# Attention products on four 64x64 quarters of TensorE's array, with q loaded like k and v

## The chip, the cores and the metric

One core of one Trainium2 chip. The metric is the time of one execution on the device in microseconds (us); lower is better. Times are medians over the runs of a kernel.

## The reference, cut to what matters

```python
# q, k, v: (8 batches, 8 heads, 576 rows, 64), float32
kv  = np.einsum('bhsd,bhse->bhde', k, v)            # a 64x64 matrix per batch and head
out = np.einsum('bhsd,bhde->bhse', q, kv)
rms = np.sqrt(np.mean(out * out, axis=-1, keepdims=True) + 1e-06)
x   = out / rms * g_norm                            # then (8*576 rows, 512 columns)
# after it: logits = x @ w_gate, a balanced routing of the 4608 rows to 8 experts
# of 576 rows each, and relu(x @ w1[e]) @ w2[e] for the rows of expert e
```

The attention comes first, then a search that settles the routing, then the experts. Only the attention (until 183 of 791 us) is touched by the change, but for a permuted index of w1 among the experts.

## The kernel before: the parts that the change and the argument touch

Two batches are a "stage". A stage makes kv of its two batches, then runs nine "tokens" (each 128 rows of output, both batches side by side) in three groups of three. The "mark" of a stage is the start of the w_ps products (kv times the gate's weights) of its second batch. A "record" is one matmul in the trace; some records can be missing. In the views PE is TensorE, DVE VectorE, ACT ScalarE and POOL GpSimd.

```python
def load_q(i):                                   # two halves of 64 partitions
    t = att.tile([P, H, R, D], FT, name="q_sb", tag="q")
    for n, eng in enumerate((nc.sync, nc.gpsimd)):
        eng.dma_start(t[n * HP:(n + 1) * HP]..., q[2 * i + n]...)

def kv_product(b):                               # two quarters: l = row and column half
    for r in range(NP):
        for j in range(R):
            for l in range(2):
                ls = slice(l * D, (l + 1) * D)
                nc.tensor.matmul(kv_ps[ls, r, :], lhsT=k_sb[ls, r, j, :], rhs=v_sb[ls, r, j, :], ...)
    nc.vector.tensor_copy(bd[0:D, b, :, 0:D], kv_ps[0:D])
    nc.scalar.copy(bd[D:P, b, :, D:P], kv_ps[D:P])
    # [cut: t_ps = transpose of bd, kvt = copy of it, w_ps = kvt times the gate, copied into bd]

def token_group(i, j0):
    nc.gpsimd.tensor_copy(q_rows, q_sb[...])
    for t in range(T):
        # [cut: 4 transposes of q_rows into qt_ps]
        nc.vector.tensor_copy(qt, qt_ps)
        for r in range(NP):
            for n in range(2):
                nc.tensor.matmul(o_ps[ps_, r, 0:W], lhsT=qt[:, r, ps_], rhs=bd[:, 2 * i + n, r], ...)
        nc.scalar.activation(sq, o_ps[...], ACT.Square, ...)
        nc.scalar.copy(o_sb[:, t], o_ps[:, :, 0:W])
        nc.vector.reduce_sum(out=ms[...], in_=sq, ...)
    # [cut: inv = 1 / rms; x_sb = o_sb * inv on GpSimd; part, lg on VectorE; write of x_sb]

for i in range(B // 2):
    for b in (2 * i, 2 * i + 1):
        kv_product(b)                            # the loads of b + 2 follow
    for j0 in range(0, R, T):
        token_group(i, j0)
        # [cut: early(...): parts of the routing that can be done by now, on VectorE]
```

## Time and profile before

| | before |
|---|---|
| median, range of 4 runs beside the changed kernel | 791.94 us, 789.05 to 792.72 |
| mean granted TensorE clock of the profiled run | 0.945 |
| second w_ps of each stage begins | 44.1, 79.8, 119.9, 153.4 us |
| first comparison of the full routing search | 183.2 us |

The prediction below reads the chain, the stretches and the groups. First, TensorE's groups in one stage, 79.80 to 119.92 us (busy us and mean ns of one, then idle time before them):

```profile
L264 PE MATMUL kv_ps<-v_sb,k_sb 64*64 64x64 f32 x288 | 12.5, 258 | 0.0
...
L288 PE MATMUL qt_ps<-ident,q_rows 128*128 128x128 f32 x36 | 5.4, 282 | 0.0
```

Second, in the waits of the same stretch, the longest (total, times, longest one):

```profile
PE t_ps L270 <- ACT bd L267: 5.0, 1, 5.0
```

Third, the granted clock in the page's 40 slices of 20 us each; the first nine digits are the attention:

```profile
PEclk9998979985569999999999999999999999999998
```

### The profile page before, as it was taken

The numbers are of one execution on the slowest core, as the hardware profiler recorded it, in microseconds if no ns is written. First come the engines' busy times: TensorE is split into PE (matmuls) and PEld (weight loads), VectorE is DVE, ScalarE is ACT, GpSimd is POOL, SyncE is SP. The second block draws the span as 40 slices with busy tenths as digits, with TensorE's granted clock in tenths as the row PEclk, the third lists the DMA queues.
The fourth block names the chain that finished last, engine by engine and source line by source line (L and its number), as shares of the span: only waits on it lengthen the run. The fifth ranks groups of instructions, "written<-read, shape, count | busy, mean of one in ns | idle before, by whom it ended". The sixth has DMA issues, their size and how long they took to land.

```text
span 791.0 us, 10903 instructions
## 1 busy us (share of the span) xinstructions
PE 681.3 (86%) x4361; PEld 443.4 (56%) x4361; DVE 344.7 (44%) x1214; ACT 151.1 (19%) x310; POOL 138.3 (17%) x118
## 2 busy tenths in 40 slices
PE   0588878951069999999999999999999999999994
PEld 0578767840047546745754674476467547646741
DVE  0364746587825625562663455165445514000000
ACT  0041504340021112102110310221031122103200
POOL 3133514230020030013003001300310032010001
PEclk9998979985569999999999999999999999999998
DMA  8999784221240080045008102600710176110001
GB/s 220 288 265 306 223 261 161 81 81 41 88 184 1 14 299 21 1 139 194 1 1 298 34 1 104 222 7 1 272 60 1 62 265 230 50 40 21 1 27 33
DMA packets 36786, 90.89 MB, mean 115 GB/s; under 512 B 2944, under 2 KB 2944, under 8 KB 36736
## 3 DMA queue, kind: packets, MB, share of 16 engines
q1 hardware_dynamic: 29056, 66.59, 25.4%
q0 software_dynamic: 6976, 23.60, 9.2%
q8 instruction: 34, 0.56, 0.3%
q10 hardware_dynamic: 704, 0.02, 0.1%
q14 instruction: 16, 0.13, 0.1%
HBM read 71.32 MB, written 18.87 MB: 114 GB/s over the span
## 4 chain that ended last, share of the span: by engine, by line
PE 59%; issue 19%; DVE 11%; DMA 5%; ACT 2%; POOL 2%; POOLq 0%; ACTq 0%; DVEq 0%
PE h_ps L552 27%; PE y_ps L563 16%; PE o_ps L295 4%; DMA v_sb<-in_v_dram 4%; PE kv_ps L264 3%; PE y_ps L571 3%; DVE part L315 2%; PE n_ps L364 1%; DVE ms L300 1%; PE qt_ps L288 1%; DVE over L238 1%; PE w_ps L275 1%; POOL out_dram L535 1%; PE t_ps L530 1%; ACT xt L531 1%
## 5 line engine op out<-in xcount | busy, mean ns | idle before, releaser
L552 PE MATMUL h_ps<-xt,w_sb 128*128 128x288 f32 x1024 | 270.8, 415 | 0.0
L563 PE MATMUL y_ps<-w_sb,hid 128*128 128x512 f32 x512 | 227.2, 597 | 0.0
L552 PEld LDWEIGHTS h_ps<-xt,w_sb 128*128 128x128 f32 x1024 | 188.8, 191 | 52.0 <-issue 5.7
L563 PEld LDWEIGHTS y_ps<-w_sb,hid 128*128 128x128 f32 x512 | 94.8, 190 | 105.2 <-issue 104.3
L535 POOL DMA_INDIRECT out_dram<-y_sb,ids x40 | 39.7, 993 | 441.3 <-ACT y_sb L566 390.7
L576 DVE TENSOR_TENSOR y_sb<-y_ps,y_part 64x512 f32<-64x512 f32 x8 | 5.5, 683 | 208.2 <-ACT y_part L575 208.2
L555 ACT ACTIVATE hid<-h_ps 128x288 f32<-128x288 f32 x128 | 52.5, 410 | 220.0 <-PE h_ps L552 218.5
L238 DVE TENSOR_TENSOR over<-mx,cand 128x1152 bf16<-128x1152 f32 (+3 forms) x52 | 67.0, 1289 | 1.6
L566 ACT COPY y_sb<-y_ps 128x512 f32<-128x512 f32 x32 | 18.7, 585 | 209.2 <-PE y_ps L563 171.7
L295 PE MATMUL o_ps<-bd,qt 128*64 128x144 f32 x576 | 46.4, 304 | 10.8 <-DVE qt L290 9.9
L506 POOL DMA_INDIRECT xg<-x_dram,ids x40 | 39.4, 986 | 83.1 <-issue 43.7
L295 PEld LDWEIGHTS o_ps<-bd,qt 128*64 128x64 f32 x576 | 38.7, 144 | 14.7 <-ACT o_sb L299 7.9
L264 PE MATMUL kv_ps<-v_sb,k_sb 64*64 64x64 f32 x1152 | 45.2, 242 | 0.1
L264 PEld LDWEIGHTS kv_ps<-v_sb,k_sb 64*64 64x64 f32 x1152 | 42.4, 156 | 3.2 <-issue 2.9
L310 POOL TENSOR_TENSOR x_sb<-o_sb,inv 128x1536 f32<-128x1536 f32 x12 | 33.2, 2768 | 50.0 <-DVE inv L308 37.0
L364 PEld LDWEIGHTS <-over 128*128 128x128 bf16 x441 | 18.1, 97 | 38.4 <-DVE over L238 22.4
L370 DVE TENSOR_TENSOR need<-goal,n_ps 32x8 f32<-32x8 f32 x49 | 7.5, 154 | 69.0 <-PE n_ps L364 69.0
L364 PE MATMUL n_ps<-best,over 128*128 128x32 bf16 x441 | 19.2, 178 | 21.4 <-DVE cand L358 12.5
L530 PE MATMUL t_ps<-ident,xg 128*128 128x128 f32 (+1 forms) x160 | 24.0, 288 | 15.3 <-issue 10.5
L385 DVE SCALAR_TENSOR_TENSOR at<-row_f,k_ps,cand 128x33 f32<-128x33 f32 x98 | 21.5, 257 | 34.3 <-PE k_ps L380 34.3
L531 ACT ACTIVATE xt<-t_ps,g_col 128x512 f32<-128x512 f32 (+1 forms) x40 | 24.0, 645 | 53.0 <-PE t_ps L530 52.9
L530 PEld LDWEIGHTS t_ps<-ident,xg 128*128 128x128 f32 (+1 forms) x160 | 18.0, 149 | 24.9 <-issue 15.1
(149 smaller groups left out, 506.4 us busy)
## 6 DMA issues: line engine op xcount, KB each, us to landing
w_sb<-in_moe_w_dram SPq DMA_DIRECT2D x16, 1024.0 KB, 6.1
w_sb<-in_moe_w_dram SPq DMA_DIRECT2D x8, 2048.0 KB, 14.2
k_sb<-in_k_dram SPq DMA_DIRECT2D x8, 1152.0 KB
v_sb<-in_v_dram SPq DMA_DIRECT2D x8, 1152.0 KB
x_dram<-x_sb SPq DMA_DIRECT2D x12, 768.0 KB, 3.3
q_sb<-in_q_dram POOLq DMA_DIRECT2D x4, 1152.0 KB
q_sb<-in_q_dram SPq DMA_DIRECT2D x4, 1152.0 KB, 27.8
xg<-x_dram,ids POOLq DMA_INDIRECT x40
```

Of the source, the lines that this page charges most:

```text
L238: nc.vector.tensor_tensor(over[:, c0:c1], mx[:, c0:c1].rearrange("p (c o) -> p c o", o=1).to_broadcast([P, c1 - c0, NCAND]), cand[:, 1:NCA ...
L264: nc.tensor.matmul(kv_ps[ls, r, :], lhsT=k_sb[ls, r, j, :], rhs=v_sb[ls, r, j, :], start=(j == 0), stop=(j == R - 1))
L295: nc.tensor.matmul(o_ps[ps_, r, 0:W], lhsT=qt[:, r, ps_], rhs=bd[:, 2 * i + n, r], start=True, stop=True)
L310: nc.gpsimd.tensor_tensor(x_sb.rearrange("p (a l d) -> p a l d", l=2, d=D), o_sb.rearrange("p t r w -> p (t r) w")[:, :, 0:P].rearrange("p ...
L364: nc.tensor.matmul(n_ps, lhsT=over[:, c:c + G].rearrange("p c n -> p (c n)"), rhs=best[:, c:c + G].rearrange("p c e -> p (c e)"), start=(c ...
L506: nc.gpsimd.indirect_dma_start(out=xg[0:nr, :], out_offset=None, in_=x_dram, in_offset=bass.IndirectOffsetOnAxis(ap=ids[0:nr, n:n + 1], ax ...
L530: nc.tensor.transpose(t_ps[:, d, 0:nr], xg[0:nr, d * P:(d + 1) * P], ident[0:nr, 0:nr])
L531: nc.scalar.mul(xt[:, :, a:a + nr], t_ps[:, :, 0:nr], g_col)
L535: put = nc.gpsimd.indirect_dma_start(out=out, out_offset=bass.IndirectOffsetOnAxis(ap=ids_of[t][0:nr, n:n + 1], axis=0), in_=y_sb[0:nr, :] ...
L552: nc.tensor.matmul(h_ps, lhsT=w1[:, d, f * P:(f + 1) * P], rhs=xt[:, d, cs], start=(d == 0), stop=(d == DC - 1))
L555: nc.scalar.activation(hid[:, f, cs], h_ps, ACT.Relu)
L563: nc.tensor.matmul(y_ps, lhsT=hid[:, f, a:a + nr], rhs=w2[:, f, :], start=(f == 0), stop=(f == FC - 1))
```

## The change

The intent: use all four 64x64 quarters at once for kv and for the output products, so that they cost half; put the same kv into both partition halves so that q can be transposed as it lies after a load over all 128 partitions; drop GpSimd's rearrangement of q and some of VectorE's copies; let x_sb start behind part and lg, one token at a time, as part was slow when it started after x_sb. The transposes of q move out of the tokens into the preparation of a batch. The core of the diff (cut: names, assertions, the same copies in another shape, and a permuted index of w1 among the experts):

```diff
-    def load_q(i):                      # two halves of 64 partitions
+    def load(name, b):                  # k, v and q alike, 128 partitions, one queue
+        nc.sync.dma_start(t.rearrange("p r j d -> p r (j d)"),
+            src[b].rearrange("h s d -> (h s) d").rearrange("(r p j) d -> p r (j d)", r=NP, j=R))
 def kv_product(b):
-                    nc.tensor.matmul(kv_ps[ls, r, :], lhsT=k_sb[ls, r, j, :], rhs=v_sb[ls, r, j, :],
+                    ls, cs = slice(l * D, (l + 1) * D), slice(j % 2 * D, (j % 2 + 1) * D)
+                    nc.tensor.matmul(kv_ps[cs, l, r * D:(r + 1) * D], lhsT=k_sb[ls, r, j, :], rhs=v_sb[ls, r, j, :],
-        nc.vector.tensor_copy(bd[0:D, b, :, 0:D], kv_ps[0:D])
-        nc.scalar.copy(bd[D:P, b, :, D:P], kv_ps[D:P])
+        nc.scalar.copy(odd, kv_ps[D:P, :, 0:NP * D])
+        nc.vector.tensor_tensor(kv, kv_ps[0:D], odd, op=AL.add)       # even and odd j
+        nc.scalar.copy(kvx[0:D, :, 0:D], kv)
+        nc.gpsimd.tensor_copy(kvx[D:P, :, 0:D], kv)                   # kv in both halves
         # t_ps, kvt, w_ps as before in other shapes
+    def turn_q(b):                      # 18 transposes of 128x128, four to a bank
 def token_group(i, j0):
-        nc.gpsimd.tensor_copy(q_rows, ...); 4 transposes and a copy per token
-        nc.gpsimd.tensor_tensor(x_sb..., o_sb..., inv...)         # three tokens at once, ahead of part
+        for t in range(T):                                        # behind part and lg
+            nc.gpsimd.tensor_tensor(x_sb[:, t], o_sb[:, t, :, 0:D], inv...)
+            for r2 in range(NP // 2):   # o products: row half by block, column half by batch
+                for l in range(2):
+                    for rp in range(2):
+                        for n in range(2):
+                            nc.tensor.matmul(o_ps[n * HP:(n + 1) * HP, rp, ...], lhsT=turned_q[...][rows, ...],
+                                             rhs=kv_of[2 * i + n][rows, 2 * r + l], ...)
 for i in range(B // 2):
     for b in (2 * i, 2 * i + 1):
         kv_product(b)
+            turn_q(b)
```

## The prediction

> **What bounds the kernel now.** I read four views: the chain of waits, the table of stretches, the groups by shape for the first 180 us, and the timeline. The chain first, because it says how much of the 791 us the change can reach at all:
>
> ```profile
> 6.84 29.95 DMA v_sb<-in_v_dram
> 36.83 4.42 PE kv_ps L264 x144
> 44.07 1.00 PE w_ps L275 x8
> ...
> 79.80 1.08 PE w_ps L275 x8
> ...
> 119.92 1.08 PE w_ps L275 x8
> ...
> 153.35 1.08 PE w_ps L275 x8
> ...
> 177.72 2.09 DVE lg L225
> 183.22 1.36 DVE over L238
> ```
>
> Columns: start, length, what. These w_ps lines are the last small products before the nine tokens of each of four stages (two batches each), so they are a clock for the attention: 44.1, 79.8, 119.9, 153.4, periods of 35.7, 40.1 and 33.5 us. It ends near 183, where the routing search starts. The 608 us after that are experts, whose code the change does not touch but for a permuted index of w1. So only some 183 us can move. Its first part is a wait for loads: kv of the second batch waits for v until 36.8.
>
> Next, what the stretches say of the loads (busy PE, then the granted clock, DMA share and GB/s at the end of each line):
>
> ```profile
> 12.00:18.00 6.00, 0.00 (x0) 0.00 (x0) 0.00 (x0) 0.00 (x0) 0.00 (x0) 1.00 1.04 244
> 72.00:78.00 6.00, 6.00 (x129) 5.74 (x129) 0.64 (x2) 0.08 (x1) 0.00 (x0) 0.70 0.97 350
> 126.00:132.00 6.00, 5.69 (x83) 4.38 (x79) 5.71 (x10) 3.99 (x8) 2.59 (x1) 1.00 0.00 0
> ```
> ```profile
> 36.83:41.17 4.34, 4.34 (x144) 4.27 (x144) 1.00 1.04 400
> 45.50:47.60 2.10, 0.00 (x0) 0.00 (x0) 1.00 1.05 193
> ```
>
> The engines are full in all but one of these, yet move 400 GB/s or 193. By issue order k and v are under way in the fast stretch and a q half in the slow one. So q is the slow load. After 126 us the DMA is idle in stretches and the last stage still takes 33 us: the late stages are bound by compute. That compute is a serial prologue (kv product, its copies and transpose, w_ps) followed by tokens, where VectorE is fullest (5.7 to 6.0 us in every stretch of 6 us inside tokens).
>
> ```profile
> L264 PE MATMUL kv_ps<-v_sb,k_sb 64*64 64x64 f32 x1152 | 45.2, 242 | 0.1
> L290 DVE COPY qt<-qt_ps 128x512 f32<-128x512 f32 x36 | 24.4, 683 | 6.4 <-PE o_ps L295 5.2 <-PE qt_ps L288 1.1
> L300 DVE TENSOR_REDUCE ms<-sq 128x8 f32<-128x512 f32 x36 | 24.3, 675 | 6.1 <-ACT sq L298 6.1
> L315 DVE TENSOR_TENSOR part<-o_sb,inv 128x192 f32<-128x192 f32 x12 | 19.7, 1640 | 0.1
> ```
> ```profile
> 143.67 0.36 DVE L315 TENSOR_TENSOR part<-o_sb,inv 128x192 f32<-128x192 f32 x1
> 143.87 2.78 POOL L310 TENSOR_TENSOR x_sb<-o_sb,inv 128x1536 f32<-128x1536 f32 x1 [3.77 <-DVE inv L308]
> ...
> 163.47 2.76 POOL L310 TENSOR_TENSOR x_sb<-o_sb,inv 128x1536 f32<-128x1536 f32 x1 [9.69 <-DVE inv L308]
> ...
> 163.75 2.69 DVE L315 TENSOR_TENSOR part<-o_sb,inv 128x192 f32<-128x192 f32 x1
> ```
>
> The last pair is worth a look: the same part takes 0.36 us when it starts before GpSimd's x_sb and 2.69 us when it starts after it. Its mean of 1.64 us is mostly waiting.
>
> **What the Trainium skill says.** "SBUF — State Buffer", section "Door 1: The DMA port swizzle": partitions 0 to 63 reach 8 of the 16 ports, measured there at 196 GB/s against 328 for 128 partitions. The trace agrees: 193 against 400 as a q half of 64 partitions or k and v of 128 are under way. The same page, "Who interferes with whom": a VectorE instruction with two SBUF inputs contends with a GpSimd instruction that reads SBUF, and whoever issues first holds the pair for the whole instruction. The 0.36 and 2.69 us above agree. "TensorEngine Tiling (Array Packing)", "Tiling Modes": 64x64 gives four tiles that work independently, and a change of mode drains the array. "TensorE: Matmul & The Clock Gate", Part 3: concurrent tiles cost about one matmul plus 4 ns for each further one. Of these the trace shows two tiles only: 144 kv records in 4.42 us, 30.7 ns each, at 218 ns recorded length.
>
> **The change part by part**, for one stage (two batches, nine tokens).
>
> *Loads.* The same 7.08 MB of k, v and q and 2.36 MB of writes. The two q halves cost about 1.18 MB / 0.195 = 6 us each; q as 128 partitions at 380 GB/s costs 3. Loads and writes now: 4.72/0.38 + 12 + about 7 = 31 us a stage; afterwards 7.08/0.38 + 7 = 26 us. At the start it is on the path. VectorE and TensorE both begin with gw, which landed at 25.6 us behind k0, v0, both q halves and k1 (5.9 MB). In the built program only k0, v0, q0 and k1 (4.7 MB) are ahead of it: 2.5 + 4.72/0.37 = about 15.3 us. v1 lands at about 19 and q1 at 22, against v1 at 36.8.
>
> *kv.* 288 records at 30.7 = 8.8 us now. On four quarters a pitch near half, 16 to 20 ns with issue cost: 5.2 us, so 3.6 us less. Added behind it on the path of each batch: the copy of the odd half on ScalarE (64x512, estimated 0.6 from the similar copies) and an add on VectorE (the 64x512 add of the experts takes 0.68), in place of two bd copies of 0.41 and 0.37. That is +0.5 a batch. The 8 w_ps records become 16 of half the columns, about equal time. kvx copies lie beside them.
>
> *q.* The 36 transposes at 0.137 remain 4.9 us of TensorE, but move from between the tokens into the prologue: the built order shows all of a batch's 18 ahead of the first full token. Of the copies out of PSUM 3 of 5 go to VectorE (0.68, 0.68, about 0.42), so 3.6 us a stage against 6.1, and 2.4 us go to ScalarE. GpSimd's q_rows copies (3 x 1.5) are gone.
>
> *Tokens.* VectorE now: 9 x (0.68 + 0.68) + 3 x (1.64 + 0.49 + about 0.86 for inverse and corrections) = 21.2 us. After: 9 x 0.68 + 3 x (0.36 + 0.49 + 0.86) = 11.2 us, because inv, part and lg stand next to each other in the built order and x_sb starts behind part. ScalarE: two passes per token start 1.02 us apart in all, 9 x 1.02 + 3 x 0.32 = 10.1 us. o_ps: 32 records of half the width on four tiles, at 20 ns 0.64 us a token, under ScalarE's pace. So tokens cost about 11 us.
>
> *One stage afterwards.* TensorE's prologue: kv 5.2, t_ps and w_ps about 3.2, q 4.9 = 13.3 us. Stalls, as the built order runs batch by batch: odd copy and add after each kv (2 x 1.5), kvt before w_ps (2 x 0.5), the first add behind the last group's chain (1): 4 to 5 us. With tokens 10 to 11: 28 us, against 33 to 40 now. DMA needs 26, so it nearly keeps up and does not bind.
>
> *Sum.* kv(0) from 15.5 to 20 (cold clock; 6.3 us now), VectorE's constants done by 21. Then add, transpose and w_ps to 24, q and kv(1) to 29, its chain and w_ps start near 32 (44.1 now). Marks at 32, 60, 88, 116. After the last mark: 16 transposes 2.2, tokens 10.5, last chain 3.5, last early choose and first search step about 5, of which the 2.1 us lg line above shrinks as x_sb is now cut into pieces of about 0.95: some 22 to 23 us where it was 29.9. End near 139, against 183: **44 us less, 792.7 - 44 = 749 us**.
>
> **Rivals.**
> 1. *The four quarters give nothing* because issue or weight loads set the pitch of 30.7 ns. For it: records of weight loads are nearly as long as the stretch (4.27 of 4.34 us). Against it: two tiles of 64 columns already run at one clock per pair near what 144 columns cost per column (32 o_ps records in 2.11 us are 66 ns, 2.15 times 30.7 for 2.25 times the columns), so the pitch follows columns, not issue. It would put back 3.6 us a stage and, as o_ps would then cost 0.98 us, little on tokens: 749 + 14 = 763.
> 2. *The bound becomes the loads*, if writes and loads queue behind each other on the one queue: three writes of a stage stand ahead of the next k load in the built order, and buffers of k and v are two. Then 30 us a stage, or 757. If instead it fills well and stalls hide, a stage falls to 25.5 and the end to 739; loads of 28.3 MB plus writes cannot do much better than 735.
> 3. *The clock.* TensorE now idles more within tokens. Before, the granted clock fell to 0.5 to 0.78 after waits, and kv of 124 records took 6.1 instead of 3.8 us. Cold prologues would add some 3 us a stage: about 760.
> 4. *Nothing comes through*, the transposes in the prologue undoing all of it: a stage of 35 us. Even then the earlier start keeps 12 us: 780, within 2%.
>
> **Range and chances.** The start (12 us) is the surest; the rest is 32 us from three stages and the end, in which each rival takes 8 to 14 and two of them may meet. I take 749, range 735 to 768. Under 777 is faster by 2%: 94%. Within 2% needs rival 4 or several together: 5%. Slower: 1%.
>
> **What would show it.** Right: first kv_ps near 16 us; GB/s of 340 to 400 in all early stretches; w_ps marks 28 us apart; kv_ps dense stretches at 16 to 20 ns a record; part at 0.36 to 0.5 us mean; qt and ms together about 11 us less VectorE; the experts' part still 608 us. Wrong: kv_ps at 30 ns (rival 1), TensorE waiting on DMA at kv_ps (rival 2), a clock under 0.8 in most of the attention (rival 3), or an experts' part that changes by more than 3 us, which nothing here explains.

## The result, and the profile after

The changed kernel takes 778.71 us (777.04 to 779.12, 4 runs) against 791.94. The ratio is 0.9836, 95% interval 0.9805 to 0.9866. A ratio here is the mean time of one kernel's fast runs over that of the other's fast runs of the same rounds, so it is not quite the ratio of the medians. About 13 us are gained, not 44; the predicted range was 735 to 768.

The start came near what was predicted. Stretches of the changed kernel (busy time of the five engines, then clock, DMA share, GB/s):

```profile
12.00:18.00 6.00, 4.41 (x146) 4.39 (x146) 4.18 (x29) 0.20 (x1) 0.00 (x0) 1.00 1.05 391
```

In this stretch the loads move 391 GB/s where it was 244, and TensorE and VectorE work where they stood still. The first kv product begins at 14.1 us (27.0 before).

The stages did not. The timeline of TensorE gives the w_ps of each stage's second batch:

```profile
31.99 0.58 PE L275 MATMUL w_ps<-gw,kvt 128*64 128x16 f32 x13 [0.59 <-ACT kvt L271]
...
69.38 1.04 PE L275 MATMUL w_ps<-gw,kvt 128*64 128x16 f32 x16
...
108.00 0.65 PE L275 MATMUL w_ps<-gw,kvt 128*64 128x16 f32 x16 [0.59 <-ACT kvt L271]
...
142.62 0.65 PE L275 MATMUL w_ps<-gw,kvt 128*64 128x16 f32 x16 [0.59 <-ACT kvt L271]
```

So the marks are 32.0, 69.4, 108.0, 142.6 where 32, 60, 88, 116 were predicted: stages of 37.4, 38.6 and 34.6 us instead of 28, and hardly different from the 35.7, 40.1 and 33.4 of before. The full search begins at 170.1 us (183.2 before), so the whole gain, 13.1 us, is the 12.1 us of the earlier first mark plus 1.0. After it nothing changed.

The stretches view of the three stages gives granted clocks of 0.81, 0.74 and 0.80. TensorE is busy in them for 25.8, 25.9 and 24.8 us. The second:

```profile
69.40:108.00 38.60, 25.93 (x642) 22.10 (x640) 21.90 (x44) 15.90 (x31) 10.69 (x11) 0.74 0.72 254
```

Where that stage goes, by TensorE's groups from 69.38 to 108.00 us:

```profile
L289 PE MATMUL qt_ps<-ident,q_sb 128*128 128x128 f32 x36 | 8.7, 413 | 0.0
L255 PE MATMUL kv_ps<-v_sb,k_sb 64*64 64x64 f32 x278 | 8.7, 260 | 0.0
L311 PE MATMUL o_ps<-kvx,qt 64*64 64x72 f32 x288 | 7.8, 245 | 4.7 <-ACT o_sb L318 4.7
...
L269 PE MATMUL t_ps<-ident,kv 64*128 64x64 f32 x8 | 1.1, 280 | 7.4 <-DVE kv L260 7.4
```

kv fell from 12.5 to 8.7 us, not to 5.2. The same 36 transposes rose from 5.4 to 8.7. TensorE stands still for 4.7 us ahead of output products and 7.4 ahead of the transpose of kv. The same view of the first and the third stage has 17.0 and 16.1 us for kv and q's transposes together, 4.6 us of waits ahead of output products in each, and 3.7 and 4.6 ahead of the transpose of kv; the second stage has the longest of these. (Overlaps make the parts of this view sum to a little more than the stage.)

The timeline shows these waits one by one (start, length, what, and in brackets the wait and what ended it):

```profile
48.33 1.24 PE L311 MATMUL o_ps<-kvx,qt 64*64 64x72 f32 x32 [2.40 <-ACT o_sb L318]
...
62.50 1.90 PE L255 MATMUL kv_ps<-v_sb,k_sb 64*64 64x64 f32 x105
...
96.04 0.68 PE L269 MATMUL t_ps<-ident,kv 64*128 64x64 f32 x4 [6.11 <-DVE kv L260]
```

The middle line is a dense stretch at a full clock: 105 records in 1.90 us, 18 ns each, inside the predicted 16 to 20. The last line is the costliest wait. VectorE's own timeline shows what it did meanwhile:

```profile
93.66 1.52 DVE L225 TENSOR_TENSOR over<-mx,cand 128x512 bf16<-128x512 f32 x1
...
95.31 0.67 DVE L260 TENSOR_TENSOR kv<-kv_ps,odd 64x512 f32<-64x512 f32 x1
```

The add that TensorE waits for (L260) stands in VectorE's program behind the last group's chain and an early part of the routing (92.26 to 95.31). Its last input, the copy odd, began at 89.98 and took 0.58 us, so it was there 4.7 us before.

And the clock, in the same slices as above:

```profile
PEclk9787777855589999999999999999999999999998
```

Sevens and eights where there were nines. A "cold" stretch is one at a granted clock near half, a "warm" one at the full clock. In a cold stretch eight q transposes take 1.97 us, in a warm one 1.09.

Three explanations offer themselves, and they do not exclude each other. **Order**: kv, the transposes and w_ps of the next stage come (but for a handful of kv products) after the tokens of this one in each engine's program, so the engines wait for each other at every seam between two stages, and each microsecond saved turns into waiting. **Clock**: the sparser TensorE runs part of the time at half rate, and loses on transposes what it gained on kv. **Loads**: two buffers of k and v keep the queue idle (7 GB/s from 42 to 48 us).

### The profile page after: what moved, and what is told of

Its sections match the earlier page's. It is cut to its first block, busy times and chain, and to the rows that moved or that the text cites. A ratio compares the mean times of both kernels' runs of the same rounds, so it can differ in the third digit from the quotient of the medians.

```text
span 777.4 us, 12187 instructions
## 1 busy us (share of the span) xinstructions
PE 659.4 (85%) x5001; PEld 420.6 (54%) x5001; DVE 329.6 (42%) x1202; ACT 164.4 (21%) x334; POOL 123.2 (16%) x132
## 4 chain that ended last, share of the span: by engine, by line
PE 51%; issue 22%; POOL 2%; DMA 2%; ACT 1%; DVE 1%; POOLq 0%; ACTq 0%
PE h_ps L572 28%; PE y_ps L583 17%; PE y_ps L591 3%; DMA xg<-x_dram,ids 2%; PE t_ps L549 1%; PE n_ps L383 1%; POOL out_dram L554 1%; ACT xt L550 1%; POOL xg L525 1%; PE k_ps L399 1%; ACT y_sb L586 0%; POOL x_sb L337 0%; DVE ms L319 0%; DVE lg L212 0%; DVE pick L216 0%
## 5 line engine op out<-in xcount | busy, mean ns | idle before, releaser
L337 POOL TENSOR_TENSOR x_sb<-o_sb,inv 128x512 f32<-128x512 f32 x36 | 37.8, 1075 | 65.8 <-DVE inv L327 34.4
L311 PE MATMUL o_ps<-kvx,qt 64*64 64x72 f32 x1152 | 31.3, 245 | 18.9 <-ACT o_sb L318 18.9
L311 PEld LDWEIGHTS o_ps<-kvx,qt 64*64 64x64 f32 x1152 | 25.1, 145 | 25.2 <-ACT o_sb L318 23.0
L383 PEld LDWEIGHTS <-over 128*128 128x128 bf16 x441 | 18.2, 97 | 36.8 <-DVE over L225 24.1
L383 PE MATMUL n_ps<-best,over 128*128 128x32 bf16 x441 | 19.2, 178 | 20.8 <-DVE cand L377 12.5
L255 PE MATMUL kv_ps<-v_sb,k_sb 64*64 64x64 f32 x1152 | 33.6, 262 | 2.5 <-DMA v_sb<-in_v_dram 2.5
L255 PEld LDWEIGHTS kv_ps<-v_sb,k_sb 64*64 64x64 f32 x1152 | 29.6, 169 | 6.7 <-issue 6.4
L289 PE MATMUL qt_ps<-ident,q_sb 128*128 128x128 f32 x144 | 32.9, 394 | 0.3 <-DVE qt L293 0.3
```

What stands on the lines that cost most here:

```text
L255: nc.tensor.matmul(kv_ps[cs, l, r * D:(r + 1) * D], lhsT=k_sb[ls, r, j, :], rhs=v_sb[ls, r, j, :], start=(j < 2), stop=(j >= R - 2))
L289: nc.tensor.transpose(t_ps[:, x, :], q_sb[:, (a + x) * P:(a + x + 1) * P], ident)
L311: nc.tensor.matmul(o_ps[n * HP:(n + 1) * HP, rp, (2 * r2 + l) * W:(2 * r2 + l + 1) * W], lhsT=turned_q[2 * i + n][rows, block // 2, l * HP ...
L337: nc.gpsimd.tensor_tensor(x_sb[:, t], o_sb[:, t, :, 0:D], inv[:, t * H:(t + 1) * H].rearrange("p (a o) -> p a o", o=1).to_broadcast([P, H, ...
L383: nc.tensor.matmul(n_ps, lhsT=over[:, c:c + G].rearrange("p c n -> p (c n)"), rhs=best[:, c:c + G].rearrange("p c e -> p (c e)"), start=(c ...
```

## The experiments

Edits are shown against the changed kernel unless said otherwise. All had three rounds beside the kernel before (medians 790.5 to 791.2 us). "Gain" is 791 us times one minus the ratio; for the changed kernel it is 13.0.

### 1. A third buffer for o_sb

```diff
-        o_sb = att.tile([P, T, H, W], FT, name="o_sb", tag="o_sb")
+        o_sb = att.tile([P, T, H, W], FT, name="o_sb", tag="o_sb", bufs=3)
```

> The changed kernel with three o_sb buffers for two; TensorE's order is the same. Theory A (the stage is a serial prologue plus tokens, with waits in it): TensorE's wait of 2.4 us at the eighth token of each stage, for o_sb held by GpSimd's x_sb, goes away: 4 x 2.4 = 9 us less, about 769 to 771, and the clock after that point is higher. Rival B (the wait only moves, to VectorE's chain or to the loads): within 2 us of 778.

Measured: 775.93 us (773.25 to 776.68), ratio 0.9797 [0.9771, 0.9824], gain 16.1. TensorE's two largest waits over three stages, 32 to 142 us, in the changed kernel:

```profile
PE t_ps L269 <- DVE kv L260: 15.7, 6, 6.1
PE o_ps L311 <- ACT o_sb L318: 13.9, 21, 2.4
```

and with the third buffer:

```profile
PE t_ps L269 <- DVE kv L260: 21.0, 6, 8.0
PE o_ps L311 <- ACT o_sb L318: 9.3, 21, 0.8
```

The wait for o_sb lost 4.6 us and the next wait in the program, for VectorE's add, grew by 5.3. The tokens ended sooner, and TensorE waited longer at the seam. That speaks for order. The time met neither expectation (769 to 771, or within 2 us of 778), and its interval overlaps that of the changed kernel (0.9805 to 0.9866), so the 3 us between them are not sure.

### 2. The writes of x on another queue

```diff
-        nc.sync.dma_start(x_dram[...], x_sb...)
+        nc.gpsimd.dma_start(x_dram[...], x_sb...)
```

> The changed kernel with the x_dram writes issued from GpSimd's queue, so that no load stands behind a write that waits for x_sb. Theory A: the 2.45 us that TensorE waits for v at 66 us goes, loads in 42 to 54 us are no longer near zero, and the time falls by 2 to 5 us to 774 to 776. Rival (the loads are not on the path): within 1 us. Against both: issuing costs GpSimd about 0.8 us a write and may delay x_sb, plus 2 us.

Measured: 778.5 us (777.3 to 779.9), ratio 0.9837 [0.9813, 0.9862], gain 12.9: nothing. k of the third stage still began to load only when kv of the stage before had been read. TensorE's wait for v stayed too (2.5 us). Writes ahead of loads on one queue are not the cause.

### 3. The kernel before with only q's load widened (wrong result)

```diff
 # against the kernel before; rows land in the wrong places
-            eng.dma_start(t[n * HP:(n + 1) * HP]..., q[2 * i + n].rearrange("h (p j) d -> p h (j d)", j=R))
+            eng.dma_start(t[:, n * NP:(n + 1) * NP]..., q[2 * i + n]...rearrange("(r p j) d -> p r (j d)", r=NP, j=R))
```

> The kernel BEFORE with only q's loads changed: each half through all 128 partitions instead of 64 (wrong result on purpose, same bytes, engines and instructions). Theory A (the 13 us gained are the earlier start by wider q loads, the rest of the change is neutral): about 779 to 782, the first mark of the stages near 34 instead of 44 us. Rival C (the loads also paced the stages before): below 775. Rival D (the start is set by gw and the number of transfers, not by their width): above 787.

Measured: 781.66 us (779.77 to 783.43), ratio 0.9872 [0.9849, 0.9896], gain 10.1. Of the 13 us of the whole change, the wide q load alone gives about 10; if the parts add, the others together gave 3. The time fits the expectation, its path only in part: the first mark came at 37.7 us (34 expected, 44.1 before, 32.0 in the changed kernel), and 3.7 us of the gain came from shorter stages after it.

### 4. Only two quarters at work at once

```diff
-            for j in range(R):
+            for j in [j for c in range(2) for j in range(c, R, 2)]:      # kv: even j, then odd j
...
-            for r2 ...: for l ...: for rp ...: for n in range(2):
+            for n, r2, l, rp in [(n, r2, l, rp) for n in range(2) ...]:   # o: one batch, then the other
```

> The changed kernel with kv's and o's products in an order in which only two quarters work at a time (same instructions, right result). If the four quarters do run together: dense kv_ps goes from 18 ns a record to about 30, o_ps from 0.73 us a token to about 1.1, and the time rises by 8 to 14 us to 786 to 792. Rival (they give nothing[...]): within 3 us of 778.

Measured: 779.78 us (775.2 to 782.44), ratio 0.9846 [0.9802, 0.9891], gain 12.2. Two dense stretches of kv:

```profile
51.85 3.04 PE L255 MATMUL kv_ps<-v_sb,k_sb 64*64 64x64 f32 x90
...
66.10 2.21 PE L255 MATMUL kv_ps<-v_sb,k_sb 64*64 64x64 f32 x98
```

The first, 34 ns a record, ran at a granted clock of 0.62; in the changed kernel 104 records at 0.65 took 2.64 us, 25 ns each. The second, at the full clock, has 23 ns where the changed kernel has 18. So two quarters cost a quarter to a third more a record, not double as expected, and less than the 30.7 ns of the kernel before: most of that fall does not come from four quarters at once, and where it comes from was not tested. A token's products take 1.04 us instead of 0.73 at the full clock.

The time rose by about 1 us, within the spread. The profile shows why the slower products cost so little: the first mark is later (35.2 us, 32.0 in the changed kernel), but from there the three stages take 108.5 us with TensorE busy for 84.9 (clock 0.76, 0.90 and 0.82), where the changed kernel takes 110.6 with 76.5. The longer busy time came out of waits. So TensorE's rate alone is not what a stage waits for.

### 5. Keeping TensorE warm

```diff
+        for _ in range(16):       # before the transpose of kv
+            nc.tensor.matmul(idle, lhsT=ones_b, rhs=inner, start=True, stop=True)          # 288 columns
...
+            for _ in range(2):    # behind each token's products, into columns that nothing reads
+                nc.tensor.matmul(o_ps[:, 0, 288:512], lhsT=ones_b, rhs=inner[..., 0:224], ...)
```

> The changed kernel with TensorE kept busy: two bf16 products of 224 columns into a part of o_ps that is overwritten or never read, behind each token's products, and sixteen of 288 columns into a spare PSUM tile in each kv product before the transpose of kv. The result stays correct. Clock theory (the faster, sparser TensorE work lets the granted clock fall, and the cold transposes, kv and o products then give back what the quarters save): the granted clock of the stages rises from 0.74-0.87 to above 0.93, eight q transposes take 1.1 us instead of 2.0, and the time falls by 6 to 12 us, to 767-773. In-order theory (the end of a stage is set by waits of VectorE and TensorE for each other in program order, not by TensorE's rate): the clock rises too, but the time stays within 4 us, 775-783, since the fillers cost about as much as warmth returns.

Measured: 776.91 us (775.28 to 778.35), ratio 0.9828 [0.9804, 0.9852], gain 13.6. The clock of the three stages rose to 0.99, 0.83 and 1.00, the mean q transpose fell from 394 to about 325 ns, and the time moved by less than 2 us. But the fillers of the first two batches delayed the first mark from 32.0 to 36.1 us, so this run was not clean, and I repeated it without them:

```diff
-        for _ in range(16):
+        for _ in range(16 if b >= 2 else 0):
```

> The changed kernel with TensorE's fillers (two small bf16 products behind each token, sixteen before the transpose of kv) but none of the sixteen in the first two batches, where they stood on the path and the first mark came at 36.1 instead of 32.0. Clock theory: first mark at 32-33, later stages as in the filler run (104 us over three stages instead of 110.6), so 770-773. If the clock is worth nothing and the filler run was only noise: 776-780.

Measured: 774.17 us (773.67 to 777.42), ratio 0.9812 [0.9784, 0.984], gain 14.9. That is 1.9 us over the changed kernel by the ratios and 4.5 by the medians, from separate calls; it falls between what the two theories expected. The three stages took 104.8 us instead of 110.6, at a clock of 0.95, 0.87 and 1.00. So warmth returned a few microseconds net. That is no upper bound of what the low clock costs: the fillers took 26 us of TensorE over the attention (12.8 and 13.3 by their groups), some of them where it would have waited, some not, and no run gives warmth without them.

### 6. Preparing the next stage between this stage's tokens

```diff
+    def prepare(b):
+        kv_product(b); turn_q(b)
+        # and the loads of b + 2
+    prepare(0); prepare(1)
     for i in range(B // 2):
-        for b in (2 * i, 2 * i + 1):
-            kv_product(b); turn_q(b)
-        for j0 in range(0, R, T):
+        for g, j0 in enumerate(range(0, R, T)):
             token_group(i, j0)
+            if g < 2 and 2 * i + 2 + g < B:
+                prepare(2 * i + 2 + g)
```

(with four buffers for kvx and qt, three for o_sb, and three for x_sb instead of six, for room)

> The changed kernel with the next stage's two kv products and q transposes written between the token groups of this stage (after the first and the second group), with four buffers for kvx and qt and three for o_sb. Same work, same instructions. In-order theory: the serial prologue (20 us between the last token product of a stage and the next w_ps mark) disappears beside the tokens; the stage period falls from 35-38 us to 26-31, what VectorE, ScalarE or the loads leave, and the time is 750-764. Clock theory: the work between tokens also keeps TensorE warm, so the run alone does not part the two, but a granted clock that stays below 0.85 together with a time under 765 would show that the clock was not it. Loads theory: the stage stays at 31 us or more with TensorE or ScalarE waiting for loads, 765-775.

Measured: 764.78 us (764.11 to 765.33), ratio 0.9669 [0.9653, 0.9685], gain 26.2, correct. The same products gain 13 us more. Not all of that is order: the third o_sb buffer alone gave about 3 (experiment 1), so some 10 remain for the order with what it needs, the further buffers of kvx and qt and the earlier loads (a batch's loads follow its preparation). TensorE waited for a load for only 2.5 us in the changed kernel, so earlier loads can hardly be the 10. The marks are 31.8, 59.8, 88.9 and 126.1: two stages of 28 and 29 us, then one of 37 in which the early routing stands in front of the add once more. The two short stages in the stretches:

```profile
32.00:60.00 28.00, 21.61 (x618) 18.60 (x617) 13.38 (x29) 13.77 (x27) 7.45 (x8) 0.84 0.77 281
60.00:89.00 29.00, 23.85 (x656) 20.78 (x657) 16.67 (x37) 15.83 (x31) 9.39 (x10) 0.80 0.85 315
```

The clock in them is 0.84 and 0.80, little above that of the changed kernel (0.81 and 0.74), so a full clock is not needed for short stages.

### 7. A third buffer for k and v (and for o_sb)

```diff
-        ... tag=name, bufs=3 if name == "q" else 2)
+        ... tag=name, bufs=3)
```

(and three buffers for x_sb instead of six, for room)

> The changed kernel with three buffers for k, v and o_sb (three for x_sb instead of six, for room). Loads theory (k(4) cannot load before kv(2) is done, so the queue is nearly idle 42-54 us and TensorE waits 2.5 us for v_sb before the w_ps mark of each stage): the wait for v_sb goes, and compared with o_sb's third buffer alone (775.9) 5 to 8 us are won, 768-771. In-order theory: the wait goes but the tokens' and VectorE's order set the stage, 773-776.

Measured: 774.23 us (773.67 to 776.6), ratio 0.98 [0.9779, 0.9821], gain 15.8: no more than o_sb's buffer alone (16.1). The expected end of the wait for v did not come (2.4 us, once, as before), because the queue now waited for q's three buffers. This run does not settle how far earlier loads could go; it shows only that a third buffer for k and v, at the price of three of x_sb, brings nothing.

### 8. Do the quarters pay once the order is right?

The edit of experiment 4 on the kernel of experiment 6.

> The version with kv and q prepared ahead (764.8), but TensorE's products ordered so that only two of the four quarters work at once (as in the run with two quarters, where kv cost 34 ns a record instead of 18-25 and a token 1.04 us instead of 0.73-1.24). If the four quarters pay once TensorE no longer stands still at the stage's end: each stage needs about 288 x 12 ns + 9 x 0.3 us = 6 us more TensorE time, of a stage of 28-29 us in which it is busy 22-24: 5 to 15 us slower, 770-780. If TensorE still has slack enough: 764-768, and the quarters are worth nothing anywhere in this kernel.

Measured: 770.76 us (770.23 to 773.28), ratio 0.9756 [0.9734, 0.9778], against 0.9669 with four quarters: 7 us slower. What made no clear difference in experiment 4 is worth 7 us here.

### 9. The same order in the kernel before

The edit of experiment 6 on the kernel before (kv products and loads only; three buffers for q).

> The kernel before with the next stage's kv products and loads written between the token groups (three buffers for q), nothing else of the change. Correct result. If the serial prologue is what hid the gain, the kernel before is held by it too, but its tokens fill VectorE (21 us a stage) and its q loads stay slow: 778-786, a gain of 5 to 13. If the prologue matters as much in it as in the changed kernel: 775-779 (14 us). If the order alone explains all of the 764.8: under 770.

Measured: 792.99 us (792.66 to 794.71), ratio 1.0025 [1.0008, 1.0042], correct. My expectation (778 to 786) was wrong: no gain at all. Its stretches suggest why:

```profile
48.00:85.00 37.00, 32.04 (x511) 27.97 (x511) 16.52 (x35) 12.80 (x25) 10.24 (x6) 0.91 0.91 252
85.00:120.00 35.00, 32.14 (x555) 27.34 (x556) 21.04 (x50) 15.06 (x29) 14.51 (x7) 1.00 0.98 316
```

TensorE is busy for 32 us of 35 to 37 and the DMA engines for over 90%: the kernel before, so ordered, has little slack to give. (Which of the two binds, no run shows; this version had no third o_sb buffer.) In these runs the order pays only together with the cheaper products and loads. The wide q load pays without the order too (experiment 3).

### 10. Two details of the reordered kernel

Two fillers of 224 columns behind each token, on experiment 6:

> The version prepared ahead with two bf16 products of 224 columns behind each token's products into columns of o_ps that nothing reads, to keep TensorE's clock up (0.80-0.84 in its stages, 0.60 in the last). Clock theory: clock above 0.9, q transposes at 1.1 us per eight instead of 1.9, 758-762. No effect of the clock: 763-768.

Measured: 766.42 us (762.83 to 768.67), ratio 0.9682 [0.9646, 0.9718]: no effect, with the clock of the three stages at 0.89, 0.92 and 0.84 (0.85, 0.80 and 0.77 without the fillers).

The early routing of 24 columns in one piece after the third stage, on experiment 6:

> The version prepared ahead with the early choice of the first 24 columns in one piece after the third stage, so that VectorE's add for kv does not stand behind it (TensorE waited 4.95 us at 119.4 and 1.7 at 105.9 for that add). In-order theory: these waits fall under 1.5 us and the third stage from 37 to 31-33 us; the time falls by 3 to 6 us, 759-762, unless the piece of choice moved to the last stage costs as much there: 764-766.

Measured: 765.4 us (763.75 to 766.25), ratio 0.9676 [0.9655, 0.9697]: no effect. The one wait of 4.95 us became one of 6.53 at the same place, as the larger piece now stood in front of the last add. The piece has to go elsewhere, or the add must not be waited for.

### 11. The next stage in small pieces between the tokens

On experiment 6: the preparation is a generator that yields after each fourth of kv and each four transposes; each token takes three pieces. q's transposes now stand between a batch's kv and the transpose of kv, so that VectorE's add has time.

```diff
     def kv_product(b):
         for r in range(NP):
             ...
+            yield
         # odd, kv, kvx
+        yield from turn_q(b)              # yields after each four transposes
         t_ps = ...
 def token_group(i, j0, ahead):
     for t in range(T):
         ...
+            for _ in range(3):
+                next(ahead, None)
```

> The version prepared ahead, but with the next stage's work cut into pieces of a fourth of a kv product or four q transposes, three pieces behind each token, and with q's transposes between a batch's kv product and the transpose of kv, so that VectorE's add has time. If what is left is waits by order (t_ps for the add, 11.6 us; stops in dense kv, 8.4 us; waits for o_sb, 6 us): these fall to under half, stages of 25-27 us, limited by loads (26) or ScalarE, and 752-760. If the stage is at the limit of TensorE's own time at this clock or of the loads: 762-766.

Measured: 753.11 us (752.9 to 754.18), ratio 0.9535 [0.9517, 0.9554], gain 36.8, correct. This is the fastest version, almost 5% below the kernel before and 3% below the changed one. It lies inside the range predicted for the change, but that is no success of the prediction, which was made for another order. Its marks in TensorE's timeline, after a first one at 30.76:

```profile
61.61 0.65 PE L278 MATMUL w_ps<-gw,kvt 128*64 128x16 f32 x16
...
90.19 0.65 PE L278 MATMUL w_ps<-gw,kvt 128*64 128x16 f32 x16
...
119.50 0.65 PE L278 MATMUL w_ps<-gw,kvt 128*64 128x16 f32 x16
```

Stages of 30.9, 28.6 and 29.3 us; the search begins at 144.8. The wait for the add is gone altogether. (I did not part the two halves of this edit, small pieces and the moved transposes.) What remains is another kind of stop:

```profile
72.74 0.90 PE L315 MATMUL o_ps<-kvx,qt 64*64 64x72 f32 x28 [4.21 <-issue]
```

"issue" means that TensorE waited for nothing that the profile shows. Such stops sum to 16.1 us between 30 and 140 us. The DMA view of the 50 ns from 70.15 us on has this line (packets, MB, share):

```profile
q8 instruction: 1, 0.02, 134.9%
```

A 16 KB packet on the queue for instructions began there (its share is over 100% because the packet is longer than the 50 ns), 2.5 us before the stop ended. This run and those of experiments 6, 8 and 9 have 22 stops without releaser of over half a microsecond; each ended 2.2 to 2.9 us after such a packet began.

### 12. Is it the number of TensorE's instructions?

On experiment 11, useless products behind each token that should take about 0.75 us of TensorE either way: 8 wide ones, or 48 tiny ones.

```diff
+            for _ in range(8):
+                nc.tensor.matmul(o_ps[:, 0, 288:512], lhsT=ones_b, rhs=inner[..., 0:224], ...)
```

> The spread version (753.1) with eight useless bf16 products of 224 columns behind each token's products (about 0.75 us of TensorE a token, 288 products more in all). TensorE theory: its time is not the bound of the stage, so little changes or up to 9 x 0.4 us a stage comes on top: 755-768. It serves as the measure for the next run.

```diff
+            for x in range(48):           # 64x64 tiles, 8 columns, on all four quarters
+                nc.tensor.matmul(o_ps[cs, (x + j0 + t) % 2, 288:296], lhsT=ones_b[rs, 0:D], rhs=inner[rs, 0, 0:8], ...)
```

> The spread version with 48 useless bf16 products of 64x64 by 8 columns behind each token's products (about 0.75 us of TensorE a token at 16 ns each, but 1728 products more in all). If TensorE's stops come from its instruction stream (a 16 KB packet holds 128 products with their weight loads by the counts of the page), there are some 13 packets more in the attention than in the run with few wide ones, with stops of 1 to 3 us at many of them: 8 to 25 us slower than it, and the stops without releaser sum to 25 us or more (16 in the spread version). If the stops have another cause: within 4 us of the run with few wide ones.

Measured: few wide 760.43 us (757.24 to 761.83), ratio 0.9619 [0.9589, 0.965]; many tiny 799.15 us (794.7 to 799.33), ratio 1.0084 [1.0043, 1.0125]: 37 us slower than few wide, where 8 to 25 were expected. By their groups the wide fillers kept TensorE busy for 34.8 us and the tiny ones for 31.9, so it is not their own time. The page's queue of instructions (packets, MB, share) with few wide ones and then with many tiny ones:

```profile
q8 instruction: 41, 0.67, 0.4%
```
```profile
q8 instruction: 53, 0.87, 0.5%
```

Without fillers there are 39 packets. 288 more products brought 2 packets and 1728 brought 14, so a packet holds some 128 products with their weight loads. TensorE's longest waits with many tiny ones, from 30 to 170 us:

```profile
PE o_ps L321 <- issue: 16.4, 8, 3.4
PE kv_ps L256 <- issue: 12.1, 7, 4.2
```

All stops without releaser sum to 34 us there, against under 5 with few wide ones. So here more instructions cost time beyond what they compute. The tiny products also ran at a lower clock (0.54 to 0.78, against 0.94 to 1.00 with the wide ones from 30 to 120 us), so not all of the 37 us need be stops. That each stop is a wait for the packet that came last is read from the times; no run took the packets away.

## Why the prediction was wrong

The first step was right in its mechanism: q was the slow load, and 391 GB/s came where 244 had been. That the first mark came at 32.0 as predicted is in part luck. gw was on the chip at 12.7 us (15.3 predicted) and kv began at 14.1 (15.5), so the chain from there to the mark took over a microsecond longer than the sum had. Experiment 3 adds that most of the 13 us needed only the wide q load.

The steps of part (mean 358 ns) and of the untouched experts were right. That loads would not bind was right (experiments 2 and 7), though they idle at times and TensorE waited for v once, for 2.5 us.

The step that failed is **"One stage afterwards"**, the sum "kv 5.2, t_ps and w_ps about 3.2, q 4.9 = 13.3 us", stalls "4 to 5 us", tokens "10 to 11: 28 us". Its shape, one part after another, is what the trace shows; its terms were too small. Stages took 37.4, 38.6 and 34.6 us. Against it stand:

- **kv and q of TensorE's prologue**, 10.1 us in the sum: 17.0, 17.4 and 16.1 us measured. This is the term that was most wrong, 20 us over three stages. It was priced as one dense run at the full clock. The dense warm rate was right (18 ns a record), but the granted clock was 0.81, 0.74 and 0.80, and in the second stage 209 of kv's records took 4.5 us in two dense stretches while the 69 others took some 4.2, in groups of 1 to 18. The prediction's own lines held a warning: kv was busy for 45.2 us over the four stages before, 11.3 a stage, where the sum put 8.8 "now".
- **Tokens**: 12.4 to 12.5 us of products and waits in each stage against 10 to 11.
- **Stalls**: with the waits for kvt 4.3, 7.4 and 5.2 us against 4 to 5, so they were near right but in the second stage. There one wait was 6.1 us, where the sum had 1.5 for the copy and add and 1 for "the first add behind the last group's chain": the chain and a part of the routing that stand ahead of the add took 4.7.

Over the three stages TensorE was busy for 76.5 us and still for 34.1. From the terms of the sum I estimate that it reckoned with some 57 and 27. The three stages are 26.6 us over the prediction, and the tail from the last mark to the search another 4.5 (27.5 against 23), together the 31 us by which the search came late.

These terms do not simply add, which the sum took for granted. Experiment 1 shortened one wait by 4.6 us and another grew by 5.3; experiment 4 made TensorE busier by 8.4 us over the three stages and they did not get longer. So what each mis-sized term cost, and how the miss splits between the low clock, the small groups and the waits, stays open; experiment 5 bounds the clock's part from below only (some 2 to 5 us net of the fillers).

What the experiments do show is what holds the built version back: its order. With the next stage's preparation between the tokens it takes 764.8 us, with two stages of 28 and 29 us at a clock of 0.84 and 0.80, and with that work in pieces 753.1. That the 24 us so recovered are near the 31 that were missing is no proof that order is what the prediction missed: it had the serial order in its sum, and the reordered versions overlap what the sum had in series.

Of the rivals, 1 (no gain from quarters) holds for the time of this version but not for its reason: the pitch did fall, from 30.7 to 18 ns, and four quarters instead of two are worth 7 us once the order is right. Rival 2 (loads) did not happen, but for the one wait of 2.5 us. Rival 3 (the clock) happened with its cold transposes; kv and q together cost 6 to 7 us a stage more than the sum had, small groups included, where it said some 3; fillers against it returned only 2 to 5 us net. Rival 4, given 5%, named the outcome (780): its reason, transposes in the prologue that undo the rest, is part of it, and its stage of 35 us is near the mean of 36.9. Its two numbers do not agree, though: in the prediction's own sum three stages of 35 us would give about 770; and the floor of 735 in rival 2 comes without its sum. Giving 94% to a gain over 2% rested on prices of TensorE's work that the lines of the kernel before did not bear out.

Open also: the rest of the way from 753 to the predicted 749. The spread version's 16 us of TensorE stops are the likeliest place, but I did not remove them.

## What to carry to other kernels

Price an engine's work as the trace of the kernel before shows it in place, in mixed small groups and at the clock that it was granted there, not by its densest stretch at the full clock; compare the price with the busy time of the group as a check. Read from the built order what each engine does at every seam: here a wait that shrank was made up by the next one (experiment 1), and what an engine had to do ahead of the awaited add set the longest wait. Order and cheaper work can be worth little apart and much together: the order gave nothing to the kernel before (experiment 9), the cheaper work 13 us, 10 of them by the wide load, and both 37 (experiment 11). Many small TensorE products had a price beyond their columns (experiment 12): count instructions too.

## What the Trainium skill lacked or had wrong

- "TensorE: Matmul & The Clock Gate", Part 3, prices packed small products by one product's duration and a few nanoseconds for each further tile, and says nothing there of the instruction stream. That is on another page: "Runtime: NRT & Kernel Launch", section "Instruction fetch mechanics", has instructions come in 16 KiB blocks of 256 and calls the cost of a block's boundary mostly hidden. The count agrees: a 16 KB packet for every 128 or so products with their weight loads. "Mostly hidden" held in the kernel before and in the changed one (stops without releaser of 0 and 0.5 us from 30 to 170 us) and not in the reordered ones (11.1 us in experiment 6, 16.1 in experiment 11) nor with 1728 tiny products (34), where stops of up to 4.2 us ended 2.2 to 3.2 us after such a packet began. Neither page says that many small products bring it out.
- The same page on TensorE, Part 1, says that TensorE's clock runs at half rate after idle windows of about 3.4 us and at full rate after as long a busy one. The trace agrees in kind: eight transposes took 1.09 us warm and 1.97 cold. What no page has is what warmth bought by fillers is worth in such a kernel: raising the clock of the stages from 0.74 to 0.81 up to 0.87 to 1.00 brought 2 to 5 us of 779, net of the fillers' own time.
